# A Strassen token mix in place of a plain one, interleaved by column group, with quarter sums

## The chip, the cores and the metric

The kernel runs on one core of one Trainium2 chip. The metric is the device time of one execution in microseconds (us), and a kernel is judged by the median of its runs. A profile is one execution recorded instruction by instruction. In it PE is TensorE (matrix products), PEld its weight loads, DVE is VectorE, ACT is ScalarE, POOL is GpSimd and SP is SyncE, which here only issues DMA transfers. "PEclk" is the clock that was granted to TensorE, as a share of the full one.

## The reference

The inputs are `x` of 8 x 4224 x 192, small weights for a causal convolution, two 192 x 192 channel matrices and two 4224 x 4224 token matrices. Everything that costs time is the token mix.

```python
x = attn_out                      # softmax-weighted causal convolution of 7 taps, 8 heads
theta = x @ w_theta
zr, zi = x * np.cos(theta), x * np.sin(theta)
y = np.einsum('ts,bsd->btd', w_tok_r, zr) + np.einsum('ts,bsd->btd', w_tok_i, zi)
u = x + y
return u + np.maximum(u @ w_ch, 0.0)
```

## The kernel before

Tokens come in 33 chunks of 128. The 8 x 192 columns of a token lie side by side, 1536 in a row. Each chunk is prepared once: convolution on TensorE, copy by ScalarE, a transposed copy (DMA, or TensorE in the first chunks), the product with `w_theta` ("theta" below) on TensorE, sine and cosine on ScalarE, and multiplication by x on VectorE. The mix then goes over the 33 output token tiles in three passes of 11 chunks each, so that only 11 chunks of zr and zi are held at a time. Partial sums between passes go to DRAM and back.

```python
def in_order(engine, ins):        # each engine executes in the order of the program
    if engine in last:
        tc.add_manual_dep(ins.ins, last[engine].ins.name, NOSYNC, reason="order")
    last[engine] = ins
    return ins
# ... cut
def transposed(u, by_pe=False):
    if not (early[0] or by_pe):
        uT = wk.tile([P, 6, P], BF16, name="uT", tag="uT")
        nc.sync.dma_start_transpose(out=uT[:, :, :], in_=u)      # issued by SyncE
        return uT
    # ... cut: six TensorE transposes, one copy by VectorE
# ... cut
def mix(y, w, zs, c, j, first=0, stop=None):      # 6534 matmuls of 512 columns in all
    cols = slice(j * PC, (j + 1) * PC)
    final = c == w.ncs - 1 if stop is None else stop
    for m in range(2):
        pe(nc.tensor.matmul(
            y, lhsT=w.wt[m][:, c, :, :].rearrange("p bt i -> p (bt i)"),
            rhs=zs[c][m][:, cols],
            start=(c == first and m == 0), stop=(final and m == 1),
        ))
# ... cut
for step in range(5):             # a chunk of the next pass, spread over this pass
    # ... cut
    if step < 2:
        ch.conv(2 * step)
        ch.conv(2 * step + 1)
        if step:
            ch.transpose(0)
            ch.transpose(1)
    elif step > 2:
        ch.theta(step - 3)
        late = (ch, step - 3)
    yield
```

The last part matters later: the transposes are issued in step 1, and TensorE needs them in step 3. Between the two it runs mix matmuls.

## Time and profile before

| | before |
|---|---|
| median of runs (lowest to highest) | 1594.13 us (1589.29 to 1597.89), 3 runs |
| span of the profiled execution | 1587.2 us |
| TensorE busy | 1562.5 us |
| VectorE busy | 814.9 us |
| mix matmuls | 6534 of 512 columns |

These are lines of the page of the kernel before: the span, the busy time of each engine, its share of the span in tenths over 40 equal slices, the chain that ended last, and two groups of instructions (out<-in, shapes, count, then busy time and mean of one in ns, then the idle time of the engine before them with what ended most of it).

```profile
span 1587.2 us, 21792 instructions
...
PE 1562.5 (98%) x8308; PEld 756.6 (48%) x8308; DVE 814.9 (51%) x1434; ACT 237.9 (15%) x379; POOL 527.3 (33%) x961
...
PE   7999999999999999999999999999999999999998
...
DVE  7962444444444444444444444445655655656554
...
PEclk9999999999999999999999999999999999999999
DMA  9966878777887898898898897768999999999993
...
PE 96%; DVE 1%; POOL 1%; DMA 1%; ACT 1%; issue 0%; DVEq 0%; ACTq 0%; POOLq 0%
...
L295 PE MATMUL y<-zr,wt 128*128 128x512 bf16 x3267 | 1240.4, 380 | 6.9 <-DVE part L436 6.2
...
L328 DVE TENSOR_TENSOR pv<-y,pv 128x512 f32<-128x512 f32 x198 | 136.9, 691 | 459.5 <-PE y L295 459.5
```

TensorE is the limit. It is busy from the second slice to the last, the chain is 96% TensorE, and VectorE, at half load, mostly waits for TensorE (459.5 us before the evictions alone). The two groups of mix matmuls overlap in this count: one takes 380 ns in the record, and in the timeline (575 to 578 us) the next one starts about 216 ns after it.

The next view is the windows of the kernel before: a stretch and its length, busy time and count of each engine in it, then granted clock, DMA share and GB/s.

```profile
0.00:100.00 100.00, 82.52 (x675) 47.57 (x676) 82.71 (x162) 57.91 (x95) 77.35 (x130) 0.98 1.00 158
100.00:1500.00 1400.00, 1399.31 (x7201) 668.33 (x7199) 686.33 (x1193) 169.88 (x268) 438.49 (x811) 1.00 0.86 171
```

### The profile page before, as it was taken

What the parts mean: (1) busy time and instruction counts of PE and PEld (TensorE: products, weight loads), DVE (VectorE), ACT (ScalarE), POOL (GpSimd) and SP (SyncE); (2) the same over time, 40 slices, a digit from 0 to 9 for tenths busy, and PEclk for the clock granted to TensorE, in tenths of its full rate; (3) what the DMA queues carried; (4) which work ended last, traced back from release to release, by engine and by line L of the source; (5) the groups of instructions that cost most, each with busy time, mean ns of one, the idle gap of its engine ahead of it and who ended that gap; (6) DMA issues with size and microseconds to landing.
All of it is one profiled execution on the core that took longest, in us unless ns stands there. A gap on an engine that the chain in (4) does not pass through costs nothing.

```text
span 1587.2 us, 21792 instructions
## 1 busy us (share of the span) xinstructions
PE 1562.5 (98%) x8308; PEld 756.6 (48%) x8308; DVE 814.9 (51%) x1434; ACT 237.9 (15%) x379; POOL 527.3 (33%) x961
## 2 busy tenths in 40 slices
PE   7999999999999999999999999999999999999998
PEld 3544444444444444444444444444444454545444
DVE  7962444444444444444444444445655655656554
ACT  5631111111111101111111110101111111111111
POOL 8742333333333333333233333223222222222220
PEclk9999999999999999999999999999999999999999
DMA  9966878777887898898898897768999999999993
GB/s 169 180 121 123 140 136 134 141 122 139 139 131 140 146 182 197 150 202 171 196 194 175 194 187 169 194 159 169 203 191 204 197 204 195 199 207 188 208 192 109
DMA packets 309640, 269.74 MB, mean 170 GB/s; under 512 B 146080, under 2 KB 281248, under 8 KB 309536
## 3 DMA queue, kind: packets, MB, share of 16 engines
q0 software_dynamic: 152256, 85.24, 45.6%
q1 hardware_dynamic: 157280, 183.12, 40.2%
q8 instruction: 65, 1.06, 0.3%
q14 instruction: 39, 0.32, 0.1%
HBM read 235.27 MB, written 90.83 MB: 205 GB/s over the span
## 4 chain that ended last, share of the span: by engine, by line
PE 96%; DVE 1%; POOL 1%; DMA 1%; ACT 1%; issue 0%; DVEq 0%; ACTq 0%; POOLq 0%
PE y L295 89%; PE v L248 5%; PE pc L165 2%; DVE zr L223 1%; PE tp L234 0%; DMA xw<-in_x_dram 0%; POOL xw L147 0%; DVE ang L198 0%; DMA st<-in_moe_w_tok_i_dram 0%; PE spare L560 0%; ACT zi L212 0%; DVE part L436 0%; ACT xz L172 0%; POOL st L267 0%; ACT zr L209 0%
## 5 line engine op out<-in xcount | busy, mean ns | idle before, releaser
L295 PE MATMUL y<-zr,wt 128*128 128x512 bf16 x3267 | 1240.4, 380 | 6.9 <-DVE part L436 6.2
L295 PE MATMUL y<-zi,wt 128*128 128x512 bf16 x3267 | 1239.5, 379 | 0.0
L295 PEld LDWEIGHTS <-wt 128*128 128x128 bf16 x6534 | 633.2, 98 | 742.8 <-issue 11.1
L267 POOL DMA_DIRECT2D st<-in_moe_w_tok_i_dram x396 | 212.8, 544 | 609.3 <-DVE wt L281 587.7
L328 DVE TENSOR_TENSOR pv<-y,pv 128x512 f32<-128x512 f32 x198 | 136.9, 691 | 459.5 <-PE y L295 459.5
L281 DVE STREAM_TRANSPOSE wt<-st 128x512 bf16<-128x512 bf16 (+1 forms) x594 | 367.9, 646 | 0.0
L267 POOL DMA_DIRECT2D st<-in_moe_w_tok_r_dram x396 | 212.8, 545 | 363.6 <-DVE wt L281 347.9
L326 DVE COPY pv<-y 128x512 f32<-128x512 f32 x87 | 60.2, 692 | 237.7 <-PE y L295 222.2
L209 ACT ACTIVATE zr<-ang,half_pi 128x768 bf16<-128x768 f32 x66 | 61.7, 935 | 521.7 <-DVE ang L198 521.7
L333 ACT ACTIVATE ub<-pv 128x512 bf16<-128x512 f32 x99 | 62.3, 630 | 480.4 <-DVE pv L328 480.4
L248 PEld LDWEIGHTS <-uT 128*128 128x128 bf16 x1056 | 91.6, 98 | 32.8 <-issue 2.1
L172 ACT ACTIVATE xz<-pc 128x384 bf16<-128x384 f32 x132 | 57.4, 486 | 312.8 <-PE pc L165 179.4
L198 DVE TENSOR_SCALAR ang<-v 128x384 f32<-128x384 f32 x132 | 67.4, 550 | 46.7 <-PE v L248 41.3
L147 POOL DMA_DIRECT2D xw<-in_x_dram x132 | 77.0, 590 | 29.1 <-PE pc L165 21.7
L351 DVE SCALAR_TENSOR_TENSOR pv<-v,pv 128x384 f32<-128x384 f32 x132 | 67.5, 553 | 4.0 <-PE v L248 1.1
L318 DVE TENSOR_TENSOR pv<-pv,xr 128x512 f32<-128x512 f32 x99 | 64.4, 650 | 0.0
L248 PE MATMUL v<-wth,uT 128*128 128x192 bf16 x528 | 55.9, 248 | 1.0 <-DVE uT L238 0.9
L212 ACT ACTIVATE zi<-ang 128x768 bf16<-128x768 f32 x66 | 54.7, 829 | 0.0
L248 PE MATMUL v<-wch,uT 128*128 128x192 bf16 x528 | 54.4, 246 | 0.0
L223 DVE TENSOR_TENSOR zr<-xz,zr 128x768 bf16<-128x768 bf16 x66 | 39.5, 611 | 0.5 <-ACT zr L209 0.5
L165 PE MATMUL pc<-xw,bands 96*64 96x192 bf16 x528 | 35.0, 252 | 0.8 <-DVE bands L536 0.5
L165 PEld LDWEIGHTS <-bands 96*64 96x64 bf16 x528 | 20.4, 109 | 28.2 <-issue 24.9
(48 smaller groups left out, 145.0 us busy)
## 6 DMA issues: line engine op xcount, KB each, us to landing
pv<-part SPq DMA_DIRECT2D x66, 768.0 KB, 5.9
part<-pv SPq DMA_DIRECT2D x62, 768.0 KB, 4.0
st<-in_moe_w_tok_r_dram POOLq DMA_DIRECT2D x396, 88.0 KB, 4.5
st<-in_moe_w_tok_i_dram POOLq DMA_DIRECT2D x396, 88.0 KB, 3.7
out_dram<-pv SPq DMA_DIRECT2D x66, 384.0 KB, 3.6
xs<-xz SPq DMA_DIRECT2D x132, 96.0 KB, 3.9
xr<-xs SPq DMA_DIRECT2D x33, 384.0 KB, 5.4
xw<-in_x_dram POOLq DMA_DIRECT2D x121, 96.0 KB, 5.1
```

The source lines that it names most:

```text
L147: nc.gpsimd.dma_start(out=self.xw[lo : lo + n, h, :, :], in_=x[:, t0 : t0 + n, :].rearrange("b s d -> s b d"),)
L165: pe(nc.tensor.matmul(pc[half * 2 * Q : (half + 1) * 2 * Q, hh * B * G : (hh + 1) * B * G], lhsT=bands[:, h, :, :].rearrange("p a m -> p ( ...
L198: dve(nc.vector.tensor_scalar(out=af[:, k * 2 * D : (k + 1) * 2 * D], in0=channel_mix(self.xT[g], k, wth), scalar1=-CLAMP, scalar2=CLAMP, ...
L209: act(nc.scalar.activation(out=self.zr[:, cols], in_=af, func=AT.Sin, bias=half_pi[:], scale=1.0))
L248: pe(nc.tensor.matmul(v[:, b * D : (b + 1) * D], lhsT=tT[:, 3 * k + b + i, :], rhs=w[:, 2 * b + i, :], start=(i == 0), stop=(i == 1),))
L267: nc.gpsimd.dma_start(out=st[a * Q : (a + 1) * Q, :, 0 : self.ncs * Q], in_=w[self.tb * P : (self.tb + 1) * P, t0 : t0 + self.ncs * Q] .re ...
L281: dve(nc.vector.transpose(self.wt[m][:, c:ce, :, :], self.st[m][:, :, c * Q : ce * Q].rearrange("p bt (c j) -> p c bt j", j=Q),))
L295: pe(nc.tensor.matmul(y, lhsT=w.wt[m][:, c, :, :].rearrange("p bt i -> p (bt i)"), rhs=zs[c][m][:, cols], start=(c == first and m == 0), s ...
L318: dve(nc.vector.tensor_tensor(out=self.pv[:, cols], in0=self.pv[:, cols], in1=self.xr[:, cols], op=ALU.add,))
L328: dve(nc.vector.tensor_tensor(out=pj, in0=y, in1=pj, op=ALU.add))
L333: nc.scalar.activation(out=self.ub[:, j * PC : (j + 1) * PC], in_=pj, func=AT.Copy)
L351: dve(nc.vector.scalar_tensor_tensor(out=pk, in0=channel_mix(uT, k, wch), scalar=0.0, in1=pk, op0=ALU.max, op1=ALU.add,))
```

## The change

The intent is to save TensorE work. The two token matrices and zr, zi are seen as 2 x 2 blocks: two output token tiles by (real, imaginary), and (real, imaginary) by (near, far half of the columns). The Winograd form of Strassen's method needs seven block products where the plain one needs eight, and pays with sums of blocks: S1 to S4 of weights, T1 to T4 of data. The 33 token tiles become 16 pairs and a lone one ("units"). A "visit" is one unit with the chunks that are held at the time. There are 61 visits, because chunks enter and leave singly. The column half of 768 is done as two groups of 384, product by product for both groups. Partial sums are kept in quarters of 768 columns in six buffers, and most reads of accumulators are on VectorE. The residual add moves to GpSimd.

The diff is 1164 lines long, nearly a rewrite; this is its core, with cuts marked.

```diff
-    PC = 512
-    PASSES = (11, 11, 11)
+    HN = N // 2
+    PC = HN // 2
+    UNITS = (NT + 1) // 2
+    SLOTS = 11
+    FIRST = (0, 0, 1, 1, 2, 3, 3, 4, 5, 6, 7)
+    dpool = ctx.enter_context(tc.tile_pool(name="dpool", bufs=6))
+    BANKS = {"y": 6, "mm": 2}
 ... cut: Visit.load, the way in of a quarter sum
+            d = pool.tile([P, HN], F32, name="d", tag=tag, bufs=n)
+            nc.sync.dma_start(out=d, in_=part[self.u][q][:, :])
+            if self.final:
+                xr = wk.tile([P, HN], BF16, name="xr", tag="xz")
+                nc.sync.dma_start(out=xr, in_=xs[self.rows(q), self.cols(q)])
+                nc.gpsimd.tensor_tensor(out=d, in0=d, in1=xr, op=ALU.add)
 ... cut: one of the seven products, and an accumulation read
+        def product(self, y, a, b, g, start=False):
+            for c in range(self.lo, self.hi):
+                pe(nc.tensor.matmul(
+                    y[:, 0:PC], lhsT=weights[self.v].block(a, c),
+                    rhs=zs[c].operand(b, g),
+                    start=(start and c == self.lo), stop=(c == self.hi - 1),
+                    skip_group_check=True,
+                ), PC)
+                yield
+                dve(nc.vector.tensor_tensor(out=o, in0=y[:, 0:PC], in1=o, op=ALU.add))
 ... cut: a visit's order; x, y, s are banks, g the column group
+            for g in gs:
+                s[g] = bank("y", "s")
+                yield self.product(s[g], "S1", "T1", g, start=True)
+                self.add(3, s[g], g, begins=True)
+            for g in gs:
+                yield self.product(y[g], "S2", "T2", g)
+                self.add(1, y[g], g, begins=True)
 ... cut: the output of a quarter
+            act(nc.scalar.activation(out=ub, in_=self.d[q], func=AT.Copy))
+            outputs.append((clock[0] + 8.0, self, q, transposed(ub, False, uT)))
 ... cut: the preparation of a chunk, in us of TensorE's program before its first use
+            (-24.0, lambda: c + 1 < NCH and c + 1 > 2 and load_chunk(c + 1)),
+            (-18.0, lambda: (chunks[c].conv(0), chunks[c].conv(1))),
+            (-15.0, lambda: (chunks[c].conv(2), chunks[c].conv(3))),
+            (-14.0, lambda: chunks[c].transpose(0)),
+            (-13.5, lambda: chunks[c].transpose(1)),
+            (-5.0, lambda: chunks[c].theta(0)),
+            (-2.5, lambda: chunks[c].theta(1)),
```

## The prediction

> **What bounds it now.** TensorE. The page's first part gives PE 1562.5 us of a 1587.2 us span, and the chain that ended last is 96% PE, 89% of it the token mix (line 295). The mix streams 6534 matmuls of 512 columns; in the timeline they start about 216 ns apart (the chain has 66 in 14.35 us).[...] So the mix is about 1409 us. Channel mixes, convolution and transposes add about 153 us (132 groups of eight at 0.86 us, 66 at 0.47 us, transposes 9 us). About 25 us is loss: some 20 us in the first 100 us, where VectorE is about 90% busy (windows) and paces the first chunks, and the end.
>
> **Removed.** Strassen (Winograd form) does 7 block products for 8 in 16 of 17 row units: 7656 matmuls of 384 columns. [...] 165 us less, all on the critical path. The 98 ns weight loads still hide. PE's own work becomes about 1397 us.
>
> **Added, mostly on VectorE**, 815 us now:
> - weight sums S1-S4, about 0.22 us per chunk and sum plus 0.15: some 195 us (estimate from the 768-element bf16 multiply, 0.55 us);
> - data sums, 132 x 0.55 = 73 us;
> - accumulation in smaller pieces and 61 visits: about 560 adds x 0.55 (the 384-element evictions) = 310 us, against 212 us now.
> The residual adds (64 us) move to GpSimd. VectorE ends near 1150-1200 us, about 80% of the new span, in strict order: no longer slack everywhere. By visit:
> - Start: an early chunk costs VectorE 7.7 us (two transposed copies 1.1, four clamps 2.2, four multiplies 2.2, four sums 2.2) where 4.9 sufficed; eleven of them, with the first weights and adds, are about 120 us, beginning near 20 us, against only about 75 us of PE work issued meanwhile. Loss about 65 us, where it was about 20.
> - Visits with 8-9 chunks and one entering: PE 21-23 us, VectorE 21.5-22.5 us each. Eleven such: loss about 15 us.
> - Last ten visits, 10 down to 1 chunks: each keeps 12 adds (6.6 us) and 8 output operations (4.4 us) while PE's work falls from 26 to 6 us; VectorE exceeds PE below six chunks, and six quarter buffers cycling through load, add, cast, transpose, mix and store hold a visit at 14-17 us (estimate). Loss about 40 us.
> Partial-sum traffic grows about 30%, weight packets about 20%; DMA share, 86-96% already, goes above 100%[...].
>
> **Sum.** 1397 + 65 + 15 + 40 = about 1517 us span, 1522 us measured. Interval 1460 to 1580. Faster by over 2%: 0.84; same: 0.13; slower: 0.03.
>
> **What would show it.** Mix matmuls 162-165 ns apart in the middle and PE fully busy in first-pass visits with 11 chunks (25 us each). VectorE over 90% busy and PE with holes in the first 150 us; PE holes growing over the last 100 us, waiting for evictions or quarter loads; VectorE 90+% between roughly 360 and 620 us.
>
> **What would make it wrong.** DMA becoming the limit in the final visits or the 8-chunk visits (weights or partial sums late): 1560 or more. GpSimd residual adds, waiting for loads, holding weight loads behind them[...]. On the good side, a start that overlaps better (visits 3 on do not need the late chunks) or a tail hidden behind its buffers: 1460.

What no trace of this case shows is cut from the prediction, and the cuts are marked. One of them takes a term out of the forecast's sum, the time of one matmul of 384 columns, on which the 165 us less rest. The sum came to 1397 + 65 + 15 + 40 = 1517 us, where 1397 is TensorE's 1562 us less those 165. The trace of the kernel before supports nearly the same by itself: three quarters of the measured 216 ns are 162 ns for 384 columns, 7656 of them 1240 us, so 169 us less than 1409 (an estimate from the 216 ns). The 98 ns of a weight load are the mean in that trace, where PEld is busy for 668.33 of the 1400 us in which TensorE idles for 0.7.

## More of the kernel before

All runs in this document were in the undisturbed (fast) state.

In the 1400 us from 100 to 1500, TensorE is idle for 0.7 us and its clock is 1.00. Whatever this kernel prepares beside the mix arrives in time. The last view of before is the timeline of one chunk's preparation (start, length, engine, instruction, count), followed by the summary of the DMA issues of those transposes, which gives the median time from issue to landing in us.

```profile
707.18 0.52 PE L165 MATMUL pc<-xw,bands 96*64 96x192 bf16 x8
...
708.48 1.72 SPq L183 DMA_DIRECT2D xs<-xz  x4
...
710.30 2.91 SPq L230 DMA_TRANSPOSE uT<-xz  x2
...
724.05 0.82 PE L248 MATMUL v<-wth,uT 128*128 128x192 bf16 x8
```

```profile
uT<-xz SPq DMA_TRANSPOSE x44, 6.3
```

The last convolution ends at 707.7. SyncE issues the two transposes 2.6 us later, and TensorE comes to theta 16.3 us after the convolution. There is no wait in brackets behind the theta line. Over all chunks prepared in this way, the first of the two transposes, which the first theta needs, landed 5.3 to 11.6 us after the convolution, and theta came at 14.2 to 16.3.

## The result, and the profile after

The prediction was wrong in sign. The kernel after is slower.

| | before | after |
|---|---|---|
| median of runs (lowest to highest) | 1595.76 us (1589.29 to 1597.89), 4 runs | 1751.24 us (1745.76 to 1755.57), 4 runs |
| span of the profiled execution | 1587.2 us | 1748.8 us |
| TensorE busy, mean granted clock | 1562.5 us, 0.997 | 1487.3 us, 0.920 |
| VectorE busy | 814.9 us | 1068.7 us |

The ratio after to before is 1.0988, with a 95% interval of 1.0955 to 1.1021. Ratios here are the mean time of one kernel's fast runs over that of the other's of the same rounds, so they are not quite the ratio of the medians quoted. The kernel before was timed once more with the kernel after, so its median differs from the one above. The result is correct.

These are lines of the page of the kernel after.

```profile
span 1748.8 us, 25577 instructions
...
PE 1487.3 (85%) x9390; PEld 904.5 (52%) x9390; DVE 1068.7 (61%) x1830; ACT 339.1 (19%) x582; POOL 703.2 (40%) x1176
...
PE   5779999999887878699999889899888878887543
...
DVE  5778544543676767576657667668656636576533
...
PEclk7689999999998989899999999999999988998865
DMA  7898766665999999977889998999889868899865
...
L405 DVE TENSOR_TENSOR d<-y,d 128x384 f32<-128x384 f32 x290 | 158.2, 552 | 238.0 <-PE y L390 188.0
...
L377 POOL TENSOR_TENSOR d<-d,xr 128x768 f32<-128x768 f32 x66 | 109.7, 1663 | 193.8 <-DMA d<-part 157.8
```

VectorE, the engine that the prediction feared, is at 61% of the span and at most 8 tenths in any slice. It too mostly waits for TensorE. TensorE has holes in the row PE, and its clock sinks in the slices with holes. The windows of the kernel after, cut where the stages begin, tell the stages apart (columns as before).

```profile
0.00:61.70 61.70, 35.46 (x231) 21.57 (x232) 38.09 (x90) 24.36 (x40) 40.84 (x86) 0.68 0.77 104
61.70:155.00 93.30, 75.67 (x526) 45.02 (x524) 73.83 (x148) 48.93 (x91) 47.38 (x87) 0.85 0.93 170
155.00:459.00 304.00, 304.00 (x1895) 183.25 (x1893) 150.99 (x214) 66.24 (x135) 110.28 (x206) 1.00 0.69 135
459.00:756.00 297.00, 241.44 (x1531) 145.15 (x1530) 198.24 (x359) 59.51 (x99) 109.19 (x200) 0.91 1.02 190
756.00:923.50 167.50, 167.50 (x1055) 101.03 (x1053) 108.34 (x167) 10.93 (x21) 56.92 (x106) 1.00 0.85 191
923.50:1244.90 321.40, 289.05 (x1854) 173.44 (x1853) 218.77 (x361) 59.35 (x100) 110.72 (x198) 0.95 0.98 184
1244.90:1461.50 216.60, 189.67 (x1206) 118.23 (x1204) 130.65 (x208) 26.78 (x37) 95.32 (x125) 0.94 0.84 177
1461.50:1748.80 287.30, 184.51 (x1108) 116.78 (x1105) 149.82 (x290) 43.00 (x61) 132.53 (x170) 0.82 0.85 183
```

Two stages are perfect: in 155 to 459 and in 756 to 923.5 TensorE has no idle time at all and clock 1.00. There a pair visit of 11 chunks takes 25.0 us for its 154 mix matmuls, and from one start to the next at clock 1.00 it is 162.5 ns on average in this trace, within the predicted 162 to 165. All of the loss lies in the other stages. I counted it by cutting the trace at the first mix matmul of each visit and taking as work 162.5 ns for each mix matmul, 0.86 us for each group of eight channel-mix matmuls and 0.47 us for each group of eight convolution matmuls. The last two figures are the prediction's. The chain of the kernel before (540 to 625 us) has 0.66 us for a group of the channel mix and 0.45 us for one of the convolution, so the count may take up to 26 us of loss for work (an estimate, 0.2 us for each of 132 groups). The start's transposes count as about 7 us of work (132 of 128 columns, an estimate at the mix's time per column), and an output's channel mix counts in the visit that it belongs to.

| stage (visits) | us | lost, predicted | lost, measured |
|---|---|---|---|
| start, to visit 4 | 0 to 155 | 65 | 77 |
| full visits, no chunk entering (4 to 16, 27 to 33) | 155 to 459, 756 to 923.5 | 0 | 0 |
| a chunk enters in each (17 to 26) | 459 to 756 | 15 | 73 |
| a chunk enters in each (34 to 43) | 923.5 to 1244.9 | 0 | 45 |
| first outputs (44 to 50) | 1244.9 to 1461.5 | 0 | 30 |
| 10 down to 1 chunk (51 to 60) | 1461.5 to 1728.4 | 40, with the end | 107 |
| after the last mix matmul | 1728.4 to 1748.8 | in the 40 | 20 |

The losses sum to 352 us; with the predicted work of 1397 us this gives 1749 us, the measured span. So the saving in work came, and 352 us of loss stand where the prediction had 120.

What TensorE waited for is in the view of waits of the kernel after (what waits, for what; us in total, times, longest).

```profile
PE v L287 <- DMA uT<-xz: 87.8, 20, 7.3
PE v L287 <- DMA uT<-ub: 46.7, 10, 6.7
PE v L287 <- DVE d L477: 40.9, 7, 8.5
PE y L390 <- DVE d L405: 18.6, 7, 6.1
```

The first is theta waiting for the transposed chunk: 55.6 us in visits 17 to 26 and 32.3 us in visits 34 to 43, and no other wait appears in those stages. The second is the output mix waiting for its transposed quarter. In the kernel before no TensorE wait adds up to more than 6.8 us. The timeline of one chunk of the kernel after shows how the first comes about; below it stands the DMA summary of the same transposes.

```profile
490.43 0.52 PE L188 MATMUL pc<-xw,bands 96*64 96x192 bf16 x8
...
491.91 0.32 SPq L373 DMA_DIRECT2D d<-part  x1
...
492.28 1.85 SPq L206 DMA_DIRECT2D xs<-xz  x4
...
494.56 0.45 SPq L411 DMA_DIRECT2D part<-d  x1
495.07 5.70 SPq L271 DMA_TRANSPOSE uT<-xz  x2
...
506.46 0.82 PE L287 MATMUL v<-wth,uT 128*128 128x192 bf16 x4 [5.49 <-DMA uT<-xz]
```

```profile
uT<-xz SPq DMA_TRANSPOSE x44, 9.4
```

The convolution ends at 490.95. Behind it SyncE has to issue, besides the four stores of x, a quarter load, a quarter store and a copy of input rows, so the first transpose starts at 495.07, 4.1 us after the convolution, and the two take 5.7 us to issue where before they took 2.9. TensorE reaches theta 10.0 us after the convolution (506.46 less the wait of 5.49, less 490.95), and there it stands. Over all such chunks the first transpose was issued 2.6 to 8.8 us after the convolution, its flight (from issue to landing) took 5.3 to 11.8 us, and the place of theta in TensorE's order was 9.9 to 10.0 us after the convolution, where the kernel before had 14 to 16. The mix matmuls behind theta in TensorE's program wait too, though none of them needs it: from 500.90 to 506.40 TensorE was busy for 0.07 us.

The waits explain 87.9 of the 118 us lost in those two stages. The rest is clock. In visit 21, whose wait was 6.3 us, the mean clock is 0.88 and the loss 8.8 us; in visit 36, whose wait was 2.5 us, the clock stays at 1.00 and the loss is 2.4 us. In the two stages the trace has 82 us at clock 0.50, 64 of them outside the waits. At clock 0.50 the mix matmuls of this kernel start 320 ns apart (median of 289), where at 1.00 they start 162.5 ns apart, so 64 us cost about 32 us, near the 30 that were to be explained. Of the 20 waits, all of 2.8 us or more and one of 2.3 us came with 3.4 or 6.8 us at clock 0.50, in the wait's end and after it; those of 0.8, 2.5 and 2.6 us did not, and neither did one of 3.2 us in visit 46, so the length of the wait alone does not tell in this trace.

The tail has its own mechanism, in the timeline of the kernel after:

```profile
1685.62 0.32 SPq L373 DMA_DIRECT2D d<-part  x1
...
1688.98 1.64 POOL L377 TENSOR_TENSOR d<-d,xr 128x768 f32<-128x768 f32 x1 [8.00 <-DMA d<-part]
...
1690.65 1.02 DVE L405 TENSOR_TENSOR d<-x,d 128x384 f32<-128x384 f32 x2 [7.68 <-POOL d L377]
...
1693.12 1.44 PE L287 MATMUL v<-wch,uT 128*128 128x192 bf16 x8 [7.49 <-DVE d L477]
```

The queue's own waits (view of waits, of the DMA queue that SyncE issues to) show what holds the load of a quarter, line 373:

```profile
SPq L373 <- DMA out_dram<-d: 122.4, 49, 7.0
```

A quarter's buffer comes free when the output of an earlier quarter has been stored. Only then does the load of the next go out; the load, the residual add on GpSimd, the add on VectorE and the output operation follow one another, and the engines behind wait 7 to 8 us. Visits 56 to 60 take 136 us for about 51 us of TensorE work.

### The profile page after: what moved, and what is told of

It is laid out like the page before. It is cut to its first block, busy times and chain, and to the rows that moved or that the text cites. A ratio compares the mean times of both kernels' runs of the same rounds, so it can differ in the third digit from the quotient of the medians.

```text
span 1748.8 us, 25577 instructions
## 1 busy us (share of the span) xinstructions
PE 1487.3 (85%) x9390; PEld 904.5 (52%) x9390; DVE 1068.7 (61%) x1830; ACT 339.1 (19%) x582; POOL 703.2 (40%) x1176
## 5 line engine op out<-in xcount | busy, mean ns | idle before, releaser
L390 PEld LDWEIGHTS <-w 128*128 128x128 bf16 x6600 | 654.8, 100 | 467.6 <-issue 68.9
L405 DVE TENSOR_TENSOR d<-y,d 128x384 f32<-128x384 f32 x290 | 158.2, 552 | 238.0 <-PE y L390 188.0
L333 DVE STREAM_TRANSPOSE w<-st 128x768 bf16<-128x768 bf16 (+5 forms) x333 | 258.8, 813 | 60.6 <-PE x L390 59.8
L390 PE MATMUL x<-zi,w 128*128 128x384 bf16 x1122 | 218.9, 350 | 0.0
L390 PE MATMUL x<-zr,w 128*128 128x384 bf16 x1122 | 203.5, 332 | 0.0
L390 PE MATMUL s<-zt,w 128*128 128x384 bf16 x1056 | 188.4, 331 | 14.9 <-DVE d L405 14.9
L390 PE MATMUL y<-zr,w 128*128 128x384 bf16 x1056 | 189.8, 331 | 13.1 <-DVE d L405 13.1
L390 PE MATMUL y<-zt,wl 128*128 128x384 bf16 x1056 | 195.4, 339 | 5.5 <-DVE d L405 5.5
L390 PE MATMUL y<-zt,w 128*128 128x384 bf16 x1122 | 197.3, 329 | 1.5 <-ACT y L423 1.4
L377 POOL TENSOR_TENSOR d<-d,xr 128x768 f32<-128x768 f32 x66 | 109.7, 1663 | 193.8 <-DMA d<-part 157.8
L390 PE MATMUL s<-zi,w 128*128 128x384 bf16 x1056 | 185.8, 330 | 0.0
L287 PE MATMUL v<-wth,uT 128*128 128x192 bf16 x528 | 70.8, 287 | 105.6 <-DMA uT<-xz 87.8
L390 PEld LDWEIGHTS <-wl 128*128 128x128 bf16 x1056 | 105.9, 101 | 79.4 <-issue 15.9
```

The costliest lines, as they stand in the source:

```text
L287: pe(nc.tensor.matmul(v[:, b * D : (b + 1) * D], lhsT=tT[:, 3 * k + b + i, :], rhs=w[:, 2 * b + i, :], start=(i == 0), stop=(i == 1),), D)
L333: dve(nc.vector.transpose(w[:, c:ce, :, :], st[:, :, c * Q : ce * Q].rearrange("p bt (c j) -> p c bt j", j=Q),))
L377: nc.gpsimd.tensor_tensor(out=d, in0=d, in1=xr, op=ALU.add)
L390: pe(nc.tensor.matmul(y[:, 0:PC], lhsT=weights[self.v].block(a, c), rhs=zs[c].operand(b, g), start=(start and c == self.lo), stop=(c == se ...
L405: dve(nc.vector.tensor_tensor(out=o, in0=y[:, 0:PC], in1=o, op=ALU.add))
```

## The experiments

There were sixteen runs with an edit. Each was timed with the kernel before in the same rounds (its medians there were 1588.7 to 1596.6 us). A diff is against the kernel after unless it says otherwise. The theory for the middle is that the transposed chunk lands after its place in TensorE's fixed order. Its rivals are that VectorE's throughput sets these visits (the prediction's view), that weight packets delay the transposes (near to a risk it named), and that GpSimd's residual adds hold VectorE up. For the tail the theory is that six quarter buffers turn over too slowly, against VectorE's throughput.

### Later use of a transposed chunk, and its rival

**e1_prepare_earlier** prepares a chunk 6 us earlier in TensorE's order, without moving theta.

```diff
-            (-24.0, lambda: c + 1 < NCH and c + 1 > 2 and load_chunk(c + 1)),
-            (-18.0, lambda: (chunks[c].conv(0), chunks[c].conv(1))),
-            (-15.0, lambda: (chunks[c].conv(2), chunks[c].conv(3))),
-            (-14.0, lambda: chunks[c].transpose(0)),
-            (-13.5, lambda: chunks[c].transpose(1)),
+            (-30.0, lambda: c + 1 < NCH and c + 1 > 2 and load_chunk(c + 1)),
+            (-24.0, lambda: (chunks[c].conv(0), chunks[c].conv(1))),
+            (-21.0, lambda: (chunks[c].conv(2), chunks[c].conv(3))),
+            (-20.0, lambda: chunks[c].transpose(0)),
+            (-19.5, lambda: chunks[c].transpose(1)),
```

> Edit: for chunks 11 to 32 everything up to the transposes (input load, convolutions, transposes) is placed 6 us earlier in TensorE's order; the clamp and all later steps stay. Theory T1 (order): TensorE waits 2 to 7 us in 21 of 22 visits because its in-order stream reaches the channel mix about 9 us after the transposes were placed, and the transposed tile lands only 8 to 12 us after its issue. With 15 us the waits on the transposed chunk (87.8 us in all, PE) should fall below 15 us, the granted clock in these visits return to 1.0, and the visits with 8 to 9 chunks take 21 to 23 us instead of 28 to 31. The visits 17 to 26 lost 73 us and 33 to 43 lost 44 us: about 100 to 117 us less, near 1640 us. Rival T2 (my prediction's own: VectorE, at 21.5 of 21 us in these visits, is the limit): VectorE's work is unchanged, so the visits with 8 chunks would still take 25 us or more and the gain would be under 50 us. Rival T3 (the DMA engines are the limit, share over 1.0 in this stage): the transposes would land later still, and the waits would only move.

It took 1693.33 us (1688.59 to 1699.47), ratio 1.0641 (1.0595 to 1.0688): 58 us better than after. The waits for `uT<-xz` fell from 87.8 to 41.5 us, and did not go. The slack in TensorE's order was now 15.9 us, as much as in the kernel before, yet transposes were issued as late as 15.1 us after the convolution. They stood in SyncE's queue behind quarter loads and stores that were themselves waiting. So the short slack is a part of the cause, and something in the queue is another.

**e2_pe_transposes** lets TensorE and VectorE transpose every chunk, so that no chunk needs the DMA. It adds 1.1 us of VectorE work for a chunk (two copies, each 556 ns in the median for the first chunks of the kernel after).

```diff
-            self.xT.append(transposed(self.xf[:, g * HN : (g + 1) * HN], self.early))
+            self.xT.append(transposed(self.xf[:, g * HN : (g + 1) * HN], True))
```

> Edit: the transposes of chunks 11 to 32 go through TensorE and a VectorE copy, as those of the first eleven do; nothing moves in the order. T1: no transposed tile can be late any more; TensorE pays 0.8 us for twelve transposes and some 1 us of waits for ScalarE and VectorE per chunk, VectorE 1.1 us more. Expect 1751 - 117 + 22 x 1.5 to 2.5 = about 1665 to 1690 us, no waits on the DMA of the transposed chunk, clock 1.0 in visits 17 to 43. T2 (VectorE the limit): with 1.1 us more of it per visit these visits take no less time than now, so 1750 us or more. T3 (DMA the limit): 44 fewer transposes lighten it; a small gain, but waits on weights or partial sums appear in their place.

It took 1637.06 us (1633.74 to 1639.93), ratio 1.0292 (1.025 to 1.0333): 114 us better than after, more than was expected and about all of the 118 us lost in visits 17 to 26 and 34 to 43. The largest wait left is one of the outputs, from the view of waits of this run:

```profile
PE v L287 <- DMA uT<-ub: 42.1, 12, 7.1
```

No line for `uT<-xz` is left. Visits 17 to 43 now take the time of their work plus 0.4 us in most of them (1.1 at most, and the 0.4 contain the new transposes), at clock 1.00. This also refutes the prediction's account of these visits, by which VectorE's throughput sets their time: VectorE had more to do, was busy for 90% of visits 17 to 26 (204.5 of 228.4 us), and TensorE was never idle there.

**e3_weights_later** tests the rival that weight packets, which come at the same time, delay the transposes. The loads go out later in the visit.

```diff
-            (0.4, lambda v=v: (start_weights(v + 2), step(v + 1), loads(v + 2, 1))),
-            (2.4, lambda v=v: (step(v + 1), loads(v + 2, 1))),
-            (2.9, lambda v=v: (step(v + 1), loads(v + 2, 1))),
-            (4.4, lambda v=v: step(v + 1)),
-            (4.9, lambda v=v: step(v + 1)),
+            (0.4, lambda v=v: (start_weights(v + 2), step(v + 1))),
+            (2.4, lambda v=v: step(v + 1)),
+            (2.9, lambda v=v: step(v + 1)),
+            (4.4, lambda v=v: (step(v + 1), loads(v + 2, 1))),
+            (4.9, lambda v=v: (step(v + 1), loads(v + 2, 1))),
+            (6.5, lambda v=v: loads(v + 2, 1)),
```

> Edit: only the issue of the token weights' loads moves, from 0.4, 2.4 and 2.9 fourteenths of a visit (when the chunk's transposes are in flight) to 4.4, 4.9 and 6.5; the order of all other work stays. It tells why the transposes land in 8 to 12 us where they took 5 to 8 in the kernel before. If it is the weight packets beside them, the transposes land in 5 to 8 us and the waits of TensorE on the transposed chunk fall from 88 to under 40 us, and the time by 50 to 90 us. If the landing time is set by other traffic (partial sums, input), the landing stays at 8 to 12 us and the time within 20 us of 1751. Weights could become late in the 8-chunk visits, which would show as TensorE or VectorE waiting for staged weights.

It took 1760.27 us (1757.58 to 1762.33), ratio 1.1059 (1.102 to 1.1098). The median from issue to landing was 9.3 us (9.4 after) and the waits for `uT<-xz` 91.0 us; the run is 9 us slower than after. The weights that were moved are not what makes the transposes late.

**e6_scalar_queue** issues the same transposes by DMA, from ScalarE's queue rather than SyncE's.

```diff
-            nc.sync.dma_start_transpose(out=uT[:, :, :], in_=u)
+            (queue or nc.sync).dma_start_transpose(out=uT[:, :, :], in_=u)
 ... cut: Chunk.transpose passes queue=nc.scalar
```

> Edit: the DMA transposes of chunks 11 to 32 are issued from ScalarE's queue instead of SyncE's; no order moves. The earlier-preparation run left waits of 41.5 us on the transposed chunk, and there the transposes were issued only 5 to 15 us after the convolution, behind loads and stores of partial sums in SyncE's in-order queue. T4 (that queue blocks the transposes): from ScalarE they are issued within 2 us of the convolution's end (now 3 to 9), land 2 to 6 us sooner, and TensorE's wait on them falls from 88 to about 30 us (the flight of 8 to 11 us stays and the slack is 10 us); time 1751 - 60 to 90 = about 1660 to 1690 us. If the flight alone is the cause (DMA engines loaded), the issue is earlier but the landing is not, and the time stays within 20 us of 1751.

It took 1669.38 us (1666.05 to 1679.15), ratio 1.0495 (1.0453 to 1.0537): 82 us better than after. One chunk in the timeline of this run:

```profile
880.68 0.52 PE L188 MATMUL pc<-xw,bands 96*64 96x192 bf16 x8
...
881.98 2.61 ACTq L272 DMA_TRANSPOSE uT<-xz  x2
...
891.05 0.82 PE L288 MATMUL v<-wth,uT 128*128 128x192 bf16 x8
```

The convolution ends at 881.20, the first transpose is issued 0.8 us later (so for 16 of the 22 chunks; for the other six 2.9 to 8.7 us), and theta finds its data. The waits for `uT<-xz` fell from 87.8 to 9.3 us, with slack and data as in the kernel after; only the queue differs. So leaving SyncE's queue is worth more than the added slack of e1. The order of that queue is fixed, and quarter loads wait in it for a buffer. In the kernel after the queue's own waits show this:

```profile
SPq L373 <- DMA part<-d: 264.3, 99, 6.8
```

Line 373 is the load of a quarter; 99 times it waited for the store that frees its buffer, up to 6.8 us, and what was behind it waited too. But the queue is not the whole cause. On average a chunk's first transpose landed 8.9 us after the convolution in the kernel before (3.0 to its issue, 5.9 in flight), 13.9 us in the kernel after (5.1 and 8.8) and 8.8 us in e6 (2.0 and 6.8). Of the 5.1 us to the issue, the waits of quarter loads for a buffer are 1.5; the four stores of x, which e6 passes by too, stood ahead in the kernel before as well. Less slack, a later issue and a longer flight together made the data late, and e6 shortened the last two. The gain of e6 is less than that of e2 by 32 us. In part that is a new wait, up to 20.7 us in all, of TensorE for copies that ScalarE now makes later. The result was correct.

### The tail

**e4_output_later** puts the output's channel mix 14 us rather than 8 us after its transpose was issued.

```diff
-            outputs.append((clock[0] + 8.0, self, q, transposed(ub, False, uT)))
+            outputs.append((clock[0] + 14.0, self, q, transposed(ub, False, uT)))
```

> Edit: the output steps of a finished quarter are placed 14 us after its transposes in TensorE's order instead of 8. T1 for the final visits: TensorE's waits on the transposed output (46.7 us in visits 45 to 55) come from the same short distance and should fall below 15 us, the loss of visits 44 to 52 from about 45 us to about 15. Against it: each quarter buffer is held 6 us longer and there are six of them; if the buffers are the limit in the last five visits (25 to 32 us each where the work is 6 to 15 us), these grow, and the sum could be zero. Net -20 to -40 us expected; a rise of the last five visits would support the buffer theory.

It took 1793.69 us (1778.7 to 1795.2), ratio 1.1249 (1.1191 to 1.1306): 42 us worse than after, where a gain was expected. The waits for `uT<-ub` fell as expected, from 46.7 to 19.2 us, but the wait for the output operations on VectorE (line 477) grew from 40.9 to 69.1 us, and visits 56 to 60 took 167 us rather than 136. That fits the buffer theory: a later output holds a quarter buffer longer.

**e7_more_quarters** gives the tail three more quarter buffers from visit 52 on, in the room that departed chunks leave.

```diff
-            pool, n = (dpool, 6) if tag == "sums" else (wk, 2)
+            pool, n = (dpool, 6) if tag == "sums" else (zpool, SLOTS + (tag == "zt"))
 ... cut
+        if vi.v == 52:
+            for tag in ("zr", "zi", "zt"):
+                free_sums(tag)
```

> Edit: from visit 52 on three more quarter buffers, in the space of chunks that are no longer used; nothing else. Theory that six quarter buffers set the pace of the last visits (visit 56 to 60 took 136 us for 51 us of TensorE work): nine buffers shorten these five visits by about a third, to 85 to 105 us, and the time falls by 30 to 50 us; the waits for additions (30 us) and for output steps (41 us) in the tail fall by half. Theory that VectorE's 11 us of fixed work per visit sets it (my prediction): VectorE was busy about a third of the time in the last 100 us, so no change under this theory would be expected from more buffers.

It took 1693.04 us (1686.88 to 1697.23), ratio 1.0621 (1.0578 to 1.0664): 58 us better than after. Visits 56 to 60 took 86 us for the same work, where they took 136. The first window is the kernel after from visit 56 to its end, the second is this run over the same work.

```profile
1592.20:1748.80 156.60, 74.45 (x403) 47.17 (x401) 68.80 (x145) 22.32 (x32) 60.53 (x72) 0.72 0.72 171
```

```profile
1595.90:1695.50 99.60, 64.25 (x404) 41.22 (x401) 69.92 (x144) 22.32 (x32) 55.79 (x70) 0.83 1.05 232
```

VectorE does the same 69 us of work in both, 44% of the longer and 70% of the shorter stretch. The number of quarter buffers set most of the loss, not VectorE, and the DMA can move more than it did (232 against 171 GB/s).

**e5_residual_on_vector** takes the residual add from GpSimd to VectorE, 7 us after the load.

```diff
-                nc.gpsimd.tensor_tensor(out=d, in0=d, in1=xr, op=ALU.add)
+                residuals.append((clock[0] + 7.0, self, q, d, xr))
 ... cut: residual_step makes the add with nc.vector when its time has come
```

> Edit: the residual additions of the final visits go back to VectorE[...] from GpSimd (1.66 us), 7 us after the loads are placed. Theory that GpSimd's share of a quarter's cycle matters in the tail: visits 56 to 60 (25 to 32 us each) shorten by 1 to 3 us each and the time falls by 5 to 15 us. Theory that the number of quarter buffers and the DMA round trip set the tail: no change beyond 5 us, or a little worse, since VectorE now waits in order for the loads. My prediction's fear that these additions hold up weight loads or VectorE's sums before visit 55: then visits 44 to 55 would get faster.

It took 1760.69 us (1750.3 to 1766.78), ratio 1.1052 (1.0999 to 1.1104). There is no gain. Visits 56 to 60 became 6 us shorter in all, as the theory of GpSimd's share has it, but TensorE's waits for accumulation reads (`y <- DVE d`) grew from 18.6 to 50.4 us, because an add that is not yet ready blocks VectorE's order. So the run doesn't price GpSimd's residual adds by themselves; e14 comes closer to that. What one add takes on VectorE: in the kernel before, 512 elements took 650 ns, which in proportion is 0.98 us for 768 (an estimate), and on GpSimd 768 took 1663 ns in the kernel after.

### The start

**e8_warm_start** keeps TensorE busy with three idle matmuls ("fillers") at each early step.

```diff
+            if t0 + off < 0:
+                events.append((t0 + off, lambda: idle(3, spare[c % 6])))
```

> Edit: three idle matmuls of 512 columns after each step of the chunks prepared before the first visit. Between 25 and 65 us the granted clock was 0.50 and no engine was busy over 65%: a chain through TensorE, ScalarE and VectorE, not VectorE's throughput as I predicted. If the halved clock stretches that chain (some 2.7 us per chunk), the first mix starts 5 to 12 us earlier than 61.7 us and the time falls as much; if VectorE's throughput is the limit, or the fillers get in the way, the first mix starts no earlier.

It took 1751.05 us (1748.87 to 1761.17), ratio 1.101 (1.0968 to 1.1053), the same as after. The clock between 20 and 60 us rose from 0.52 to 0.91, but the first mix matmul came at 74.0 us rather than 61.7. But the run does not acquit the half clock. Between 20 and 74 us TensorE executed 115 fillers, which at 216 ns each (the spacing of 512 columns in the kernel before) are 25 us of its time, an estimate, so the fillers may have hidden a gain. Whether the half clock sets the pace of the start stays open.

**e9_early_banks** lets the early chunks use the six accumulator banks that lie idle at the start, rather than two.

```diff
-            pc = bank("mm", "pc")
+            pc = bank(fill[0], "pc")
 ... cut: the same for tp and v; fill[0] is "y" until the first visit, then "mm"
```

> Edit: the chunks prepared before the first visit take their accumulation banks from the six that the visits use later, not from the two for small products. In the start each chunk takes 10.9 us (convolution to convolution); the fillers showed that the halved clock is not what sets that. What is left is the chain through two banks: TensorE waits for clamps behind four sums (1.7 us), the convolution waits for ScalarE (1.6 us), VectorE waits 3.5 us for the next transposes. If the banks are what closes the chain, a chunk takes about 8.5 us, the first mix starts near 52 us instead of 62 and the time falls by 5 to 10 us. If it is the fixed order on VectorE and ScalarE, the first mix stays within 3 us of 62.

The result was wrong (relative error 0.0323); the time still tells something. It took 1745.29 us (1736.73 to 1750.88), ratio 1.094 (1.089 to 1.099), with the first mix matmul at 59.7 us, 2 us earlier than after, so banks are at most a small part of it. The cause of the error was not shown. The kernel copies the first product from bank x into bank y with ScalarE and lets a later product accumulate on it. In the kernel after the idle matmuls had written whole banks before that; in this run narrower groups used them in between. No run here tells whether that matters.

**e13_early_order** changes only the order of an early chunk's parts: both thetas first, then the four waves, then the multiplies, so that ScalarE's and VectorE's fixed orders wait less for one another.

```diff
-            (4.5, lambda: (chunks[c].theta(0), chunks[c].wave(0, 0), chunks[c].wave(1, 0))),
-            (6.0, lambda: (chunks[c].theta(1), chunks[c].wave(0, 1), chunks[c].wave(1, 1))),
-            (7.5, lambda: (chunks[c].times_x(0, 0), chunks[c].times_x(1, 0))),
-            (8.5, lambda: (chunks[c].times_x(0, 1), chunks[c].times_x(1, 1))),
-            (9.5, lambda: [chunks[c].sum(i) for i in range(4)]),
+            (4.5, lambda: chunks[c].theta(0)),
+            (5.5, lambda: chunks[c].theta(1)),
+            (7.2, lambda: [chunks[c].wave(i, g) for g in range(2) for i in range(2)]),
+            (9.2, lambda: (chunks[c].times_x(0, 0), chunks[c].times_x(1, 0))),
+            (9.4, lambda: (chunks[c].times_x(0, 1), chunks[c].times_x(1, 1))),
+            (11.7, lambda: [chunks[c].sum(i) for i in range(4)]),
```

> Edit, in the kernel after the change: of the first eleven chunks only the order of the steps changes: both clamps, then the four waves after the next chunk's convolutions, the multiplies after its transposes, the four data sums after its clamps. No work is added or removed. If the fixed order on ScalarE and VectorE closes the chain (in the trace ScalarE copies a convolution only behind four waves, and VectorE clamps only behind four sums), a chunk takes 8 to 9 us instead of 10.9, the first mix starts near 50 us instead of 62, visit 4 starts 15 to 30 us earlier than 155, and the time falls as much, to about 1720 to 1735. If VectorE's throughput is the limit (7.7 us a chunk with 71% busy says it is not), or the loads, visit 4 starts within 5 us of 155.

It took 1733.98 us (1722.41 to 1739.28), ratio 1.0893 (1.0851 to 1.0934): 17 us better than after. The first mix matmul came at 55.3 us (61.7 after) and visit 4 began at 140.2 us (155.0 after). VectorE was busy for 31.0 of the 40 us from 20 to 60 (24.3 after). The same VectorE work fits in less time, so order was a part of the start's loss, at an unchanged clock of 0.52. About 60 us of that loss remain, and their cause stays open.

### The mends together

**e10_both_mends** is e2 and e7 in one kernel (a line of each, shown above).

> Edit: transposes of chunks 11 to 32 on TensorE, and three more quarter buffers from visit 52: the two largest mends together. They act in separate visits (17 to 43, and 55 to 60), so they should add: 114 + 58 = 172 us below 1751, about 1579 us, ratio to the kernel before 0.99. If DMA load or VectorE tied them together, the sum would be missed by more than 15 us.

It took 1584.92 us (1582.73 to 1592.78), ratio 0.9948 (0.991 to 0.9985). The two gains add up to within 6 us: 114 and 58 from 1751 give 1579.

**e11_output_on_pe** is e10 with the outputs transposed on TensorE too, 3 us after the cast, and mixed 3 us after that.

```diff
-            outputs.append((clock[0] + 8.0, self, q, transposed(ub, False, uT)))
+            outputs.append([clock[0] + 3.0, self, q, ub, uT, False])
 ... cut
+    def turn(o):
+        o[4] = transposed(o[3], True, o[4])
+        o[5], o[0] = True, clock[0] + 3.0
```

> Edit: the one before, and the finished quarters are also transposed on TensorE, 3 us after the last product, with the output mix 3 us after that (8 us after a DMA transpose now). The waits on the transposed output (60 us in all in the run with more quarters) should vanish, at 0.4 us of TensorE and 0.55 us of VectorE per quarter; visits 44 to 52 lost 45 us and should lose under 10, a quarter's cycle in the tail gets some 5 us shorter. About 1579 - 40 to 60 = 1520 to 1540 us, ratio 0.955 to 0.965.

It took 1571.13 us (1568.47 to 1572.09), ratio 0.9854 (0.9821 to 0.9887): 14 us better than e10, less than was expected. Visits 45 to 48 now take 31.0 us, 2.5 more than their work as counted above, but visits 51, 54 and 57 lose 11, 7 and 8. At the start of visit 51 the profiled run is 18 us ahead of e10's and at its end 16, so the tail gained nothing.

**e12_all** is e11 with the banks of e9.

> Edit: the one before, with the early banks of the first run of this set. If those help alone, the same 5 to 10 us here: 1512 to 1532 us; if not, as the one before.

Its result was wrong by the same error as that of e9. It took 1569.81 us (1565.68 to 1571.5), ratio 0.984 (0.9809 to 0.9871), no different from e11, which again says that banks matter little at the start.

**e14_late_residual** is e11 with GpSimd's residual adds placed 7 us after their loads, so that weight loads issued by GpSimd don't stand behind an add that waits.

```diff
-                nc.gpsimd.tensor_tensor(out=d, in0=d, in1=xr, op=ALU.add)
+                residuals.append((clock[0] + 7.0, self, q, d, xr))
 ... cut: residual_step makes the add with nc.gpsimd when its time has come
```

> Edit, on the run with outputs transposed on TensorE (1571 us): GpSimd's residual additions are placed 7 us after the loads that they wait for instead of with them, so that weight loads go ahead of them in GpSimd's order. If that order delays weights (VectorE waited 3.3 us for a staged weight tile in visit 53, then all else), the visits 51, 54 and 57 (losses of 11, 7 and 8 us) lose under 4 each and the time falls by 10 to 20 us. If the losses come from the quarter buffers or VectorE, no change beyond 5 us.

It took 1570.97 us (1567.39 to 1571.57), ratio 0.9873 (0.9847 to 0.99). Visits 51 and 57 lose 2.3 and 1.8 us where they lost 11 and 8, but 54 still loses about 6, visits 56, 58 and 60 lose more, and the sum did not change. So the place of GpSimd's residual adds shifts losses between visits here, and in this pair of runs it does not change the time. They did hold VectorE up at times: a VectorE sum of 128 x 768 bf16 took about 0.55 us alone and 3.44 us while two of GpSimd's residual adds ran (e11, at 1433.15 us). Over a whole execution such stretching came to about 10 us in the kernel after and 15 us in e11 (an estimate: what VectorE's instructions that ran beside those adds took over the median of their kind), so it was not what made the kernel slow.

**e15_best** is e11 with the order of e13, and **e16_best_late** is e15 with the placing of e14.

> Edit: the run with outputs transposed on TensorE, with the early order. The start acts alone, so the gain of the order run should be had whole: 1571 - 15 to 30 = 1541 to 1556 us, ratio 0.967 to 0.976: a clear win over the kernel before.

> Edit: the one before, with the late residual additions. If both help, 1525 to 1545 us; if the late additions do nothing, as the one before within 5 us.

e15 took 1557.87 us (1549.53 to 1563.09, 6 runs), ratio 0.9791 (0.9763 to 0.9819): its interval lies on both sides of a gain of 2%, so the verdict is unclear and not the clear win that was expected. e16 took 1549.3 us (1548.77 to 1550.81, 5 runs), ratio 0.9743 (0.9718 to 0.9769), and its result is correct. It missed its expectation of 1525 to 1545 narrowly, and its gain of 9 us over e15, where the same edit gave e14 nothing, is not explained. So the changed kernel's arithmetic does beat the kernel before, by 2.6%, once its transposes, buffers and early order are mended. In e16 visits 17 to 43 run at clock 1.00 and within 1.3 us of their work each; most of what it still loses is in the start and in visits 52 to 60.

## Why the prediction was wrong, point by point

- **TensorE bounds the kernel before:** right. It was idle for 0.7 of 1400 us.
- **"PE's own work becomes about 1397 us":** right. The expected 162 to 165 ns from one mix matmul to the next are met by 25.0 us for 154 of them. The sum of this work and the counted losses is the measured span.
- **"Visits with 8-9 chunks and one entering: ... VectorE 21.5-22.5 us each ... loss about 15 us":** this is the step that failed first. The stage was priced by adding up what each engine has to do. VectorE's work was sized well (19.8 us a visit in the kernel after) but was not the limit (e2 gave it more work and lost nothing). The limit was a latency: the transposed chunk landed after its place in TensorE's fixed order. The loss in visits 17 to 26 was 73 us. The same happened in visits 34 to 43, for which the prediction had no loss at all, with 45 us. Three things made it late. Two were to be read in the diff: the place of theta, 9.9 us behind the convolution where it had been 14 to 16 (e1: 58 us when put back), and SyncE's queue, in which quarter loads wait for buffers ahead of the transposes (e6: 82 us when bypassed). The third is a flight 2.9 us longer on average, whose cause is open. The effects overlap; without the DMA transposes of chunks the run gains 114 us (e2).
- **The named risk, "DMA becoming the limit ... (weights or partial sums late)":** near, but not it. TensorE never waited for weights in these visits, and moving their loads did not help (e3). The partial sums mattered as what stands first in a queue.
- **Visits 44 to 50, no loss predicted:** 30 us, by the same step. The output's transpose had 8 us in TensorE's order; the waits for `uT<-ub` in this stage are 25.1 us. With these transposes on TensorE the visits 44 to 50 lose 12 us, by the same count, where e10 lost 30 (e11).
- **"six quarter buffers cycling ... hold a visit at 14-17 us (estimate). Loss about 40 us":** the mechanism was right and its size off. Visits 56 to 60 took 23.3 to 32.5 us each. With nine buffers they took 12.0 to 21.2 (e7). The prediction's other reason for the tail, that VectorE exceeds TensorE below six chunks, was right as a count of work (68.8 us busy against about 51 us of TensorE work) but did not set the time: VectorE was busy for 44% there.
- **"Loss about 65 us" at the start:** the size was nearly right (77), the reason only in part. VectorE was to be over 90% busy; it was at 61% from 20 to 60 us and at 75% from 100 to 150. A fixed order of two engines that wait for one another is 15 to 17 us of it (e13). The banks are at most a small part (e9), and e8 does not tell whether the half clock is one. The rest is open.
- **"VectorE ends near 1150-1200 us, about 80%":** 1068.7 us, 61% of a longer span.
- **The sum:** "1397 + 65 + 15 + 40" became 1397 + 77 + 73 + 45 + 30 + 107 + 20. Of the 232 us that the losses exceed the predicted 120, the middle has 103 (73 + 45 less 15), the first outputs 30, the tail and the end 87 (107 + 20 less 40), and the start 12.
- **Half clock after a gap** was not in the prediction at all. In visits 17 to 26 and 34 to 43, with 64 us at clock 0.50 outside the waits, it accounts for the difference between 118 us lost and 87.9 us waited.

What stays open is why a transpose's flight took longer in the kernel after (median over both of a chunk's transposes 9.4 us from issue to landing, 3.2 to 11.8; before 6.3, 2.7 to 9.1; 7.1 from the other queue), the rest of the start, and the rest of the tail. The mean load of the DMA engines does not explain the flight alone: the first transposes of chunks 22 and 20 flew 5.3 and 11.8 us while the DMA share was 1.28 and 1.29.

## What to carry to other kernels

When engines execute in a fixed order, sum the busy times to find the bound, and then check each transfer that TensorE will need: how long after its source it is needed in TensorE's order, and what stands ahead of it in its issuing queue. Here a queue that held loads waiting for a buffer was the wrong place for a transfer that TensorE needed within 10 us. Where a stage has few matmuls for each buffer, count the buffers that turn over in it, and place the critical ones first.
